# The head of an S5 state-space plus SwiGLU kernel: one activation for the inverse deviation, gate and up weights loaded three feature tiles at a time, and the second chunk of x held back by a GpSimd write

## The chip, the cores and the metric

The kernel runs on one core of a Trainium2 chip. A core has TensorE (PE, matrix products; PEld is its weight load, which overlaps the products), VectorE (DVE), ScalarE (ACT), GpSimd (POOL) and SyncE (SP, which here only issues DMAs). Sixteen DMA engines carry the transfers that SP, ACT and POOL issue, each from its own queue. The metric is the device time of one execution in microseconds (us); the profile shows one execution and its span, which leaves out a little around the work.

## The reference

The input x has 2048 rows of 512 numbers in bf16. It is layer-normalized, and the output is the sum of x and two branches on the normalized rows xn:

```python
xn = _layernorm(x, axis=-1)                       # (x - mean) / sqrt(var + 1e-5)
return x + A(xn) + B(xn)

# A: diagonal complex state space, 512 states
dt = exp(log_dt); Lam = Lambda_re + 1j * Lambda_im
Lam_bar = exp(dt * Lam);  B_bar = ((Lam_bar - 1.0) / Lam)[:, None] * (B_re + 1j * B_im)
h_t = Lam_bar * h_(t-1) + B_bar @ xn_t
y_t = 2.0 * real(Cmat @ h_t) + xn_t * Dskip

# B: feed-forward with 1376 features
(silu(xn @ w_gate) * (xn @ w_up)) @ w_down
```

## The kernel before

**Tiling.** The rows are 16 token tiles of 128 (`NT`), in four chunks of 512 (`CW`, four tiles each, `TPC`). The 512 columns are four slices of 128 (`KD`). The 1376 features are ten tiles of 128 and a last one of 96. `xnT` holds xn transposed, the moving operand of all products on the input side. A gate or up product of a feature tile and a chunk is four matmuls of 512 columns (one per slice), a tile of the state space's input (`bproj_tile`, stationary operand `BT`, real part and imaginary part) is four as well.

**The head.** For chunk 0 the work goes token tile by token tile, so that TensorE can start before all of x is there: `ln_stats` (DVE: bn_stats and bn_aggr, variance and mean), `rstd_act` (ACT: Ln and Exp, lines 206 and 207), `norm_dve` (DVE, line 219), `xT_pe` (four TensorE transposes by an identity, line 236, and two copies from PSUM on DVE or ACT, lines 243 and 245), then `head_mm` (line 696): gate and up matmuls of 128 columns of the first three feature tiles, gathered in six PSUM banks (`held`). `dummy` issues matmuls on ones to keep TensorE busy before there is work. After the head, `gu_out` applies Silu on ACT and copies the up half. The order is written out by hand; each engine runs its instructions in the order of the code and waits by semaphores.

**After the head.** Feature tiles 3 to 6 of chunk 0 (line 448), the eight `bproj_tile`s of chunk 0 (line 373), feature tiles 7 to 9 and the last one, then chunk 1 and so on. Beside that, a backlog of DVE and ACT work (`queue`, `pump`, `need`) is handed out by estimated costs: the layer norm of the next chunk (tag ln1: four statistics, a power on POOL for rstd, four normalizations, each followed by a DMA transpose), the sine and cosine tables (`table_ops`), the scans.

**Loads.** `fgroups` cuts the gate and up weights into groups of feature tiles, (0, 2), (2, 3), (3, 7), (7, 10), each one tile in SBUF (`wg0`, `wu0` and so on) with one DMA (`load_w1`, line 112). SP's queue issues in this order: x tile 0, gate group 0, x tile 2, gate and up group 1, x tiles 4 to 7 in two DMAs (line 137), gate and up group 2, the four DMA transposes of B's real part (line 142), gate and up group 3, the four of its imaginary part, the last feature tile's weights, then the DMA transposes of chunk 1 (line 250) and the later loads. ACT's queue issues x tile 1, up group 0, x tile 3. POOL's queue loads the three parameter rows of the state space. A DMA is issued only when the earlier one that used its semaphore has landed.

**Parameters.** `prm_transpose` (in `xT_pe(2)`) turns the three parameter rows, `params_a` and `params_a2` compute dt = exp(log_dt) and r = exp(dt * Lambda_re) on ACT and load the table for Silu and Sin, `params_sin` reduces angles to turns on DVE and takes two sines on ACT.

Of the kernel before, what the change touches and what calls it, by code (L numbers as in the profile page):

```python
# [10 lines left out]
F32 = mybir.dt.float32  # L11
# [5 lines left out]
MAGIC = 12582912.0  # L17
# [6 lines left out]
def kernel(  # L24
# [63 lines left out]
    fgroups = [(0, 2), (2, 3), (3, 7), (7, FT - 1)]  # L88
# [41 lines left out]
    load_w1(nc.sync, wg_g, wg_v, 1)  # L130
    load_w1(nc.sync, wu_g, wu_v, 1)
# [4 lines left out]
    for n in (TPC, TPC + 2):  # L136
        nc.sync.dma_start(out=xall[:, n:n + 2, :], in_=x_v[:, n:n + 2, :])
    load_w1(nc.sync, wg_g, wg_v, 2)
    load_w1(nc.sync, wu_g, wu_v, 2)
    for part, src in enumerate((A_B_re, A_B_im)):  # L140
        for k in range(KD):
            nc.sync.dma_start_transpose(out=BT[:, part, k, :], in_=src[:, k * 128:(k + 1) * 128])
        if part == 0:
            load_w1(nc.sync, wg_g, wg_v, 3)
            load_w1(nc.sync, wu_g, wu_v, 3)

    nc.sync.dma_start(out=w_last[:, :, 0:LB + LA], in_=wg_v[:, :, FL:F])
    nc.sync.dma_start(out=w_last[:, :, LB + LA:128], in_=wu_v[:, :, FL + LB:F])

# [38 lines left out]

    stats = const.tile([128, NT, 6], F32, name="stats")
    mv = const.tile([128, NT, 2], F32, name="mv")  # L190
# [13 lines left out]
    def rstd_act(n):  # L204

        nc.scalar.activation(out=ve[:, n:n + 1], in_=mv[:, n, 1:2], func=ACT.Ln, bias=eps_t[:, 0:1])
        nc.scalar.activation(out=rstd[:, n:n + 1], in_=ve[:, n:n + 1], func=ACT.Exp, scale=-0.5)
# [9 lines left out]
    def norm_dve(n):  # L217
        c, i = divmod(n, TPC)
        nc.vector.tensor_scalar(out=xn_tile(c)[:, i, :], in0=xall[:, n, :], scalar1=mv[:, n, 0:1],  # L219
                                scalar2=rstd[:, n:n + 1], op0=ALU.subtract, op1=ALU.mult)  # L220
# [93 lines left out]
    def params_sin():  # L314

        def turns(dst, shift):
            src = ws2[:]
            if shift:
                V.tensor_scalar(out=dst[:], in0=src, scalar1=shift, scalar2=None, op0=ALU.add)
                src = dst[:]  # L320
            V.tensor_scalar(out=kk[:], in0=src, scalar1=MAGIC, scalar2=MAGIC, op0=ALU.add, op1=ALU.subtract)
            tt(dst[:], src, kk[:], ALU.subtract)

        V.tensor_scalar(out=ws2[:, 1, :], in0=ws2[:, 0, :], scalar1=float(CW), scalar2=None, op0=ALU.mult)
        turns(fs1, 0.0)
        nc.scalar.activation(out=sin1[:], in_=fs1[:], func=ACT.Sin, scale=TWO_PI_LO)
        turns(fc1, 0.25)
# [554 lines left out]
```

## Time and profile before

| | |
|---|---|
| median of 3 runs | 179.12 us (179.03 to 179.21) |
| profiled execution | 179.15 us, of which its span 177.4 us |
| busy share of the span | PE 97%, DVE 87%, ACT 53%, PEld 47%, POOL 21% |
| chain that ended last | PE 96%, DMA 1%, DVE 1% |
| granted TensorE clock | full |
| read and written in HBM | 8.42 MB and 5.24 MB, 77 GB/s over the span |

The busy share of an engine is an average over the whole span. The chain that ended last follows the work back from the last instruction, at each step to what released it. A line of the timeline gives the start, the length, the engine, the line of the code, the operation, what is written and read, how many instructions are merged, and in brackets how long the engine sat idle before and what ended that. PEq, SPq and ACTq are the sequencers that issue. An issue on SPq is only the issue: the transfer lands later, and the table of DMA issues gives the time from issue to landing.

### The profile page before, as it was taken

How to read it: one execution, taken by the hardware profiler on the slowest of the kernel's cores; microseconds unless marked ns; L12 is line 12 of the kernel's file. 1: busy time of each engine (PE TensorE's matmuls, PEld its weight loads, DVE VectorE, ACT ScalarE, POOL GpSimd, SP SyncE). 2: the span in 40 equal slices, each digit the busy share in tenths (PEclk: the TensorE clock that was granted, in tenths of full speed). 3: DMA queues.
4: the chain of work that ended last, by engine and by line, in shares of the span. 5: the costliest groups of instructions: out<-in, count | busy, mean ns of one | idle time of the engine just before them, and what ended most of it. 6: DMA issues, size and time to landing. Idle time of an engine off the chain costs nothing.

```text
span 177.4 us, 2512 instructions
## 1 busy us (share of the span) xinstructions
PE 172.8 (97%) x921; PEld 83.0 (47%) x921; DVE 154.8 (87%) x239; ACT 94.8 (53%) x173; POOL 37.6 (21%) x57
## 2 busy tenths in 40 slices
PE   7899999999999999999999999999999999999993
PEld 2784444444444444444444444444444444464443
DVE  6789997999999977899999999999999999992033
ACT  3579696977399459924966662013866610001300
POOL 6003000001200040000706640005183720001410
PEclk9999999999999999999999999999999999999999
DMA  5999748983041025900460011005569600000662
GB/s 158 311 274 239 147 90 245 342 135 89 0 89 33 0 40 107 355 0 0 43 79 9 15 51 42 0 0 59 59 79 184 113 8 0 0 0 4 64 103 71
DMA packets 30092, 16.13 MB, mean 91 GB/s; under 512 B 19296, under 2 KB 29888, under 8 KB 30048
## 3 DMA queue, kind: packets, MB, share of 16 engines
q1 hardware_dynamic: 24416, 11.41, 28.1%
q0 software_dynamic: 4416, 3.87, 16.1%
q10 hardware_dynamic: 1248, 0.69, 1.4%
q8 instruction: 7, 0.11, 0.3%
q14 instruction: 5, 0.04, 0.1%
HBM read 8.42 MB, written 5.24 MB: 77 GB/s over the span
## 4 chain that ended last, share of the span: by engine, by line
PE 96%; DMA 1%; DVE 1%; issue 0%
PE ps L448 36%; PE ps L608 16%; PE ps L373 16%; PE ps L561 10%; PE ps L589 10%; PE ps L696 3%; PE ps L503 2%; DMA xall<-in_A_x_dram 1%; PE ps L492 1%; PE ps L596 1%; PE ps L549 1%; PE ps L236 1%; DVE stats L201 0%; DVE stats L703 0%; DVE xall L219 0%; DVE res L613 0%
## 5 line engine op out<-in xcount | busy, mean ns | idle before, releaser
L448 PE MATMUL ps<-xnT,wu 128*128 128x512 bf16 x148 | 38.0, 379 | 0.0
L448 PE MATMUL ps<-xnT,wg 128*128 128x512 bf16 x148 | 38.0, 379 | 0.0
L415 DVE TENSOR_TENSOR_SCAN g<-r_t,car,u 128x512 bf16<-128x512 f32 x24 | 28.8, 1262 | 0.0
L373 PE MATMUL ps<-xnT,BT 128*128 128x512 bf16 x128 | 28.3, 379 | 0.0
L608 PE MATMUL ps<-CF,wt 128*128 128x512 bf16 (+2 forms) x144 | 28.2, 355 | 0.0
L462 ACT ACTIVATE guT<-ps 128x512 bf16<-128x512 f32 x40 | 24.6, 615 | 5.0 <-PE ps L448 4.9
L463 ACT CAST u<-ps 128x512 bf16<-128x512 f32 x40 | 24.1, 601 | 5.2 <-PE ps L448 5.0
L620 ACT CAST res<-ps 128x512 bf16<-128x512 f32 x12 | 6.8, 594 | 37.5 <-PE ps L608 37.5
L621 POOL DMA_DIRECT2D out_dram<-res x12 | 10.7, 1062 | 59.4 <-ACT res L620 59.4
L448 PEld LDWEIGHTS <-wu 128*128 128x128 bf16 x148 | 14.5, 98 | 17.5
L448 PEld LDWEIGHTS <-wg 128*128 128x128 bf16 x148 | 14.5, 98 | 17.2
L608 PEld LDWEIGHTS <-wt 128*128 128x128 bf16 x144 | 13.3, 98 | 14.9 <-issue 0.8
L375 ACT CAST u<-ps 128x512 bf16<-128x512 f32 x32 | 17.7, 589 | 3.6 <-PE ps L373 3.6
L373 PEld LDWEIGHTS <-BT 128*128 128x128 bf16 x128 | 12.5, 98 | 15.1
L589 PE MATMUL ps<-wd_sb,guT 128*128 128x512 bf16 x80 | 18.1, 379 | 0.0
L561 PE MATMUL ps<-wd_sb,guT 128*128 128x512 bf16 (+1 forms) x90 | 17.6, 355 | 0.0
L211 POOL TENSOR_TENSOR rstd<-ve,neg_half 128x4 f32<-128x4 f32 x3 | 5.3, 1763 | 54.1 <-DVE ve L210 54.1
L186 POOL DMA_DIRECT2D gu_rows<-gu_last x24 | 12.0, 506 | 10.3 <-DVE gu_last L479 9.0
L467 DVE TENSOR_TENSOR guT<-guT,u 128x1024 bf16<-128x1024 bf16 x20 | 13.5, 679 | 0.0
L561 PEld LDWEIGHTS <-guT 128*128 128x128 bf16 x90 | 8.8, 98 | 8.7
L589 PEld LDWEIGHTS <-guT 128*128 128x128 bf16 x80 | 7.8, 97 | 9.5
L613 DVE TENSOR_TENSOR res<-ps,xn_end 128x512 bf16<-128x512 f32 (+1 forms) x4 | 2.5, 625 | 10.6 <-PE ps L608 10.6
(116 smaller groups left out, 196.1 us busy)
## 6 DMA issues: line engine op xcount, KB each, us to landing
out_dram<-in_A_x_dram SPq DMA_DIRECT2D x1, 1536.0 KB, 7.1
out_dram<-res POOLq DMA_DIRECT2D x12, 128.0 KB, 3.2
out_dram<-xall POOLq DMA_DIRECT2D x3, 512.0 KB, 7.8
wd_sb<-in_B_w_down_dram SPq DMA_DIRECT2D x1, 1280.0 KB, 10.2
xall<-in_A_x_dram SPq DMA_DIRECT2D x1, 1024.0 KB, 6.5
xall<-in_A_x_dram SPq DMA_DIRECT2D x2, 256.0 KB, 4.7
wg<-in_B_w_gate_dram SPq DMA_DIRECT2D x1, 512.0 KB, 5.4
wu<-in_B_w_up_dram SPq DMA_DIRECT2D x1, 512.0 KB, 6.3
```

The lines of the kernel that those rows point to most:

```text
L186: nc.gpsimd.dma_start(out=gu_rows[c % 2][i * RT:(i + 1) * RT, p, :], in_=gu_last[c % 3][p * RT:(p + 1) * RT, i * 128:(i + 1) * 128])
L373: nc.tensor.matmul(ps[:], lhsT=BT[:, part, k, q * 128:(q + 1) * 128], rhs=xnT[:, k, c * CW:(c + 1) * CW], start=(k == 0), stop=(k == KD - 1))
L375: nc.scalar.copy(out=u_tiles[c][:, part, q, :], in_=ps[:])
L415: V.tensor_tensor_scan(out=g()[:, part, q, :], data0=r_t[:, q:q + 1].to_broadcast([128, CW]), data1=u_tiles[c][:, part, q, :], initial=ini ...
L448: nc.tensor.matmul(ps[:fs, lo:hi], lhsT=wslice(groups, fi, k), rhs=xnT[:, k, c * CW + lo:c * CW + hi], start=(k == 0), stop=(k == KD - 1))
L462: nc.scalar.activation(out=guT[:fs, fi, :], in_=psg[:fs], func=ACT.Silu)
L463: nc.scalar.copy(out=u_pair[c][:fs, fi % 2, :], in_=psu[:fs])
L467: products.append(lambda: V.tensor_tensor(out=g, in0=g, in1=u, op=ALU.mult))
L561: nc.tensor.matmul(o[:, lo:hi], lhsT=gu_tiles[k][:, fi, i * 128:(i + 1) * 128], rhs=wd_sb[:, fi, lo:hi], start=(fi == 0), stop=False)
L589: nc.tensor.matmul(o[:], lhsT=gu_tiles[c][:, fi, i * 128:(i + 1) * 128], rhs=wd_sb[:, fi, lo:hi], start=(fi == 0), stop=False)
L608: nc.tensor.matmul(o, lhsT=w_tiles[c][:, part, q, i * 128:(i + 1) * 128], rhs=CF[:, part, q, lo:hi], start=(fresh and part == 0 and q == 0 ...
L621: nc.gpsimd.dma_start(out=out_v[:, n, :], in_=res[:], accum_op=ALU.add)
```

## The change

- The head's rstd is one ACT instruction, Abs_reciprocal_sqrt of the variance with the epsilon as bias, in place of Ln and Exp; the activation table loaded at the start is another, and the table for Silu and Sin is loaded right after the head's last rstd.
- The first weight groups are (0, 3), (3, 7), (7, 10): three feature tiles in the first gate load and in the first up load, no loads of a single tile. The head computes all three feature tiles token tile by token tile.
- x tile 1's statistics are taken in two halves, with tile 0's normalization between them. Eight dummies of 512 columns and two of 128 stand in place of nine of 512.
- Token tiles 4 to 7 are loaded by four DMAs, and they come behind a GpSimd write of two numbers, read from gate group 0, into the place of tile 4; so SP issues tile 4, and all that stands behind it in its order, when gate group 0 has landed.
- The two exponentials of the parameters are powers of e on GpSimd, the parameter transpose moves from `xT_pe(2)` to `xT_pe(3)`, the turns (`params_turns`) are the first item of the tables in the backlog, the two sines a later one.

```diff
-    fgroups = [(0, 2), (2, 3), (3, 7), (7, FT - 1)]
+    fgroups = [(0, 3), (3, 7), (7, FT - 1)]
...
-    eps_t = const.tile([128, 1], F32, name="eps_t")
-    nc.vector.memset(eps_t[:], EPS)
-    nc.scalar.preload_act_table_set("natural_log_exp_and_others")
+    nc.scalar.preload_act_table_set("abs_reciprocal_sqrt_and_small")
...
     nc.sync.dma_start(out=xall[:, 2, :], in_=x_v[:, 2, :])
     nc.scalar.dma_start(out=xall[:, 3, :], in_=x_v[:, 3, :])
-    load_w1(nc.sync, wg_g, wg_v, 1)
-    load_w1(nc.sync, wu_g, wu_v, 1)
...
-    for n in (TPC, TPC + 2):
-        nc.sync.dma_start(out=xall[:, n:n + 2, :], in_=x_v[:, n:n + 2, :])
-    load_w1(nc.sync, wg_g, wg_v, 2)
-    load_w1(nc.sync, wu_g, wu_v, 2)
...
+    e_t = const.tile([128, NQ], F32, name="e_t")
     ident = const.tile([128, 128], BF16, name="ident")
     make_identity(nc, ident[:])
+    nc.gpsimd.memset(e_t[:], float(np.e))
...
+    nc.gpsimd.tensor_copy(out=xall[0:1, TPC, 0:2], in_=wg_g[0][0:1, 0, 0:2])
+    for n in range(TPC, 2 * TPC):
+        nc.sync.dma_start(out=xall[:, n, :], in_=x_v[:, n, :])
+    load_w1(nc.sync, wg_g, wg_v, 1)
+    load_w1(nc.sync, wu_g, wu_v, 1)
+    for part, src in enumerate((A_B_re, A_B_im)):
+        for k in range(KD):
+            nc.sync.dma_start_transpose(out=BT[:, part, k, :], in_=src[:, k * 128:(k + 1) * 128])
+        if part == 0:
+            load_w1(nc.sync, wg_g, wg_v, 2)
+            load_w1(nc.sync, wu_g, wu_v, 2)
...
     def rstd_act(n):
-        nc.scalar.activation(out=ve[:, n:n + 1], in_=mv[:, n, 1:2], func=ACT.Ln, bias=eps_t[:, 0:1])
-        nc.scalar.activation(out=rstd[:, n:n + 1], in_=ve[:, n:n + 1], func=ACT.Exp, scale=-0.5)
+        nc.scalar.activation(out=rstd[:, n:n + 1], in_=mv[:, n, 1:2], func=ACT.Abs_reciprocal_sqrt, bias=EPS)
...
     def params_a(pp):
         V.tensor_copy(out=prm[:].rearrange("p t q -> p (t q)"), in_=pp[:, 0:3 * NQ])
-        nc.scalar.activation(out=dt_t[:], in_=ldt, func=ACT.Exp)
-    def params_a2():
-        V.tensor_tensor(out=dre[:], in0=dt_t[:], in1=lre, op=ALU.mult)
-        nc.scalar.activation(out=r_t[:], in_=dre[:], func=ACT.Exp)
-        nc.scalar.preload_act_table_set("silu_and_others")
+        nc.gpsimd.tensor_tensor(out=dt_t[:], in0=e_t[:], in1=ldt, op=ALU.pow)
+        nc.gpsimd.tensor_tensor(out=dre[:], in0=dt_t[:], in1=lre, op=ALU.mult)
+        nc.gpsimd.tensor_tensor(out=r_t[:], in0=e_t[:], in1=dre[:], op=ALU.pow)
+    def params_turns():
...
         V.scalar_tensor_tensor(out=ws2[:, 0, :], in0=dt_t[:], scalar=INV_2PI, in1=lim, op0=ALU.mult, op1=ALU.mult)
+        V.tensor_scalar(out=ws2[:, 1, :], in0=ws2[:, 0, :], scalar1=float(CW), scalar2=None, op0=ALU.mult)
+        turns(fs1, 0.0)
+        turns(fc1, 0.25)
...
     allk = range(KD)
-    dummy(9, CW)
+    dummy(8, CW)
+    dummy(2, 128)
     ln_stats(0)
     rstd_act(0)
-    nc.vector.bn_stats(out=stats[:, 1, :], in_=xall[:, 1, :])
+    nc.vector.bn_stats(out=stats_1[:, 0, :], in_=xall[:, 1, 0:D // 2])
     norm_dve(0)
-    nc.vector.bn_aggr(out=mv[:, 1, :], in_=stats[:, 1, :])
+    nc.vector.bn_stats(out=stats_1[:, 1, :], in_=xall[:, 1, D // 2:D])
+    nc.vector.bn_aggr(out=mv[:, 1, :], in_=stats_1[:])
     rstd_act(1)
     xT_pe(0, on_dve=(0,))
     dummy(4, 128)
     norm_dve(1)
     ln_stats(2)
-    head_mm(0, 0, 1, range(0, HK), (0, 1))
-    head_mm(0, 0, 1, range(HK, KD), (0, 1))
+    kh = (range(0, HK), range(HK, KD))
+    fis = range(H)
+    head_mm(0, 0, 1, kh[0], fis)
+    head_mm(0, 0, 1, kh[1], fis)
     xT_pe(1)
     rstd_act(2)
-    head_mm(1, 0, 1, range(0, HK), (0, 1))
-    head_mm(1, 0, 1, range(HK, KD), (0, 1))
+    head_mm(1, 0, 1, kh[0], fis)
+    head_mm(1, 0, 1, kh[1], fis)
...
     rstd_act(3)
-    head_mm(0, 1, 2, range(0, HK), (0, 1))
-    head_mm(1, 1, 2, range(0, HK), (0, 1))
-    head_mm(0, 1, 2, range(HK, KD), (0, 1))
-    head_mm(1, 1, 2, range(HK, KD), (0, 1))
-    head_mm(0, 0, 2, allk, (2,))
-    pp = xT_pe(2, on_dve=(0, 1), prm_too=True)
-    head_mm(1, 0, 2, allk, (2,))
+    nc.scalar.preload_act_table_set("silu_and_others")
+    head_mm(0, 1, 2, kh[0], fis)
+    head_mm(0, 1, 2, kh[1], fis)
+    xT_pe(2, on_dve=(0, 1))
+    head_mm(1, 1, 2, allk, fis)
     norm_dve(3)
+    head_mm(0, 2, 3, kh[0], fis)
+    head_mm(1, 2, 3, kh[0], fis)
+    pp = xT_pe(3, on_dve=(0, 1), prm_too=True)
     params_a(pp)
-    params_a2()
...
-    queue("tables", tables[:2])
+    queue("tables", [(1.0, params_turns)] + tables[:2])
     queue("ln1", norm1)
-    queue("tables", tables[2:])
+    queue("tables", tables[2:4] + [(0.1, params_sin)] + tables[4:])
```

More of the change, by code (lines that the diff above doesn't have):

```diff
@@ L187, in move_rows @@
                                     in_=gu_last[c % 3][p * RT:(p + 1) * RT, i * 128:(i + 1) * 128])
+    nc.gpsimd.tensor_copy(out=xall[0:1, TPC, 0:2], in_=wg_g[0][0:1, 0, 0:2])
[9 more added lines that the diff above has]
+            load_w1(nc.sync, wu_g, wu_v, 2)
+    nc.sync.dma_start(out=w_last[:, :, 0:LB + LA], in_=wg_v[:, :, FL:F])
+    nc.sync.dma_start(out=w_last[:, :, LB + LA:128], in_=wu_v[:, :, FL + LB:F])
     stats = const.tile([128, NT, 6], F32, name="stats")
+    stats_1 = const.tile([128, 2, 6], F32, name="stats_1")
     mv = const.tile([128, NT, 2], F32, name="mv")
@@ L215, in ln_nb, with norm_dve @@
                                        op0=ALU.mult, op1=ALU.mult)
-    def norm_dve(n):
+    def norm_dve(n, lo=0, hi=D):
         c, i = divmod(n, TPC)
-        nc.vector.tensor_scalar(out=xn_tile(c)[:, i, :], in0=xall[:, n, :], scalar1=mv[:, n, 0:1],
+        nc.vector.tensor_scalar(out=xn_tile(c)[:, i, lo:hi], in0=xall[:, n, lo:hi], scalar1=mv[:, n, 0:1],
                                 scalar2=rstd[:, n:n + 1], op0=ALU.subtract, op1=ALU.mult)
```

33 lines of the change are left out of this document (9 added, 24 removed).

## The prediction

> **What bounds the kernel now.** I read the page's shares first (PE busy 97% of the span), then the chain that ended last in order of time, because a share cannot say where the other 3% lies.
>
> ```profile
> 5.11 0.40 PE ps L236 x4
> ...
> 5.78 0.62 PE ps L696 x8
> ...
> 12.09 6.91 PE ps L448 x32
> 18.99 6.91 PE ps L373 x32
> ```
>
> Columns: start, length, what. Before these lines the path is the load of the first x tile, its statistics and normalization up to 5.06, and from 5.11 TensorE alone until 174.6. Whatever starts TensorE earlier is won in full; whatever makes it wait anywhere later is lost in full.
>
> Second, the timeline around the first normalization, which is what the new rstd touches:
>
> ```profile
> 4.08 0.29 ACT L206 ACTIVATE ve<-mv,eps_t 128x1 f32<-128x1 f32 x1 [2.06 <-DVE mv L202]
> 4.41 0.20 ACT L207 ACTIVATE rstd<-ve 128x1 f32<-128x1 f32 x1
> 4.64 0.41 DVE L219 TENSOR_SCALAR xall<-xall,mv,rstd 128x512 bf16<-128x512 bf16 x1
> ```
>
> Third, SP's issues, and the table of DMA issues (last column: microseconds from issue to landing):
>
> ```profile
> 3.24 1.81 SPq L137 DMA_DIRECT2D xall<-in_A_x_dram  x2
> 5.09 0.47 SPq L112 DMA_DIRECT2D wg<-in_B_w_gate_dram  x1
> 5.84 0.37 SPq L112 DMA_DIRECT2D wu<-in_B_w_up_dram  x1
> 6.25 5.76 SPq L142 DMA_TRANSPOSE BT<-in_A_B_re_dram  x4
> ...
> 12.57 0.75 PEld L448 LDWEIGHTS <-wu 128*128 128x128 bf16 x4
> ```
> ```profile
> wg<-in_B_w_gate_dram SPq DMA_DIRECT2D x1, 512.0 KB, 5.4
> wu<-in_B_w_up_dram SPq DMA_DIRECT2D x1, 512.0 KB, 6.3
> wg<-in_B_w_gate_dram SPq DMA_DIRECT2D x1, 384.0 KB, 4.6
> wu<-in_B_w_up_dram SPq DMA_DIRECT2D x1, 384.0 KB, 6.1
> ```
>
> The up weights of tiles 3 to 6 are issued at 5.84 and land at 12.1; TensorE loads the first of them at 12.57. That slack of 0.4 to 0.5 us is the narrowest on the input side, and the loads are bound by bandwidth (337 to 349 GB/s from 7 to 11 us). Last, slices of half a microsecond (us, busy time of PE, PEld, DVE, ACT, POOL, clock, DMA share, GB/s) and the instruction queue of the slice from 12.3 to 12.4:
>
> ```profile
> 12.00:12.50 0.50, 0.50 (x5) 0.22 (x3) 0.47 (x3) 0.50 (x2) 0.00 (x0) 1.00 1.44 291
> 12.50:13.00 0.50, 0.50 (x4) 0.20 (x2) 0.47 (x3) 0.50 (x2) 0.00 (x0) 1.00 5.39 168
> 13.00:13.50 0.50, 0.50 (x4) 0.26 (x3) 0.50 (x2) 0.50 (x2) 0.00 (x0) 1.00 0.02 2
> 13.50:14.00 0.50, 0.50 (x4) 0.23 (x3) 0.47 (x3) 0.50 (x2) 0.00 (x0) 1.00 0.08 9
> 14.00:14.50 0.50, 0.50 (x4) 0.19 (x2) 0.47 (x2) 0.50 (x2) 0.00 (x0) 1.00 0.71 154
> ```
> ```profile
> q8 instruction: 1, 0.02, 68.2%
> ```
>
> At 12.35 TensorE's instruction stream is refilled by one 16,384-byte packet, and from 12.78 to 14.23 nearly nothing moves, with transposes in the queue. At 17.21 another instruction fetch is followed, from 17.66 to 18.58, by 8 GB/s; the 384 KB up load whose last data packet started at 17.2 landed only at 18.8 (the 6.1 above). At 34.27 a third is followed by a standstill from 35.1 to 36.8. Before the change all three fall where TensorE waits for nothing.
>
> **The change, part by part.** The profiled run took 179.15 us with a span of 177.4; the median shown is 179.12, so I sum against 179.15 and lower the result by 0.03.
>
> *One activation for rstd.* Ln and Exp cost 0.29 and 0.20, and with hand-overs 4.08 to 4.61. One activation lies between these rows, done at 4.31 to 4.40; I take 4.40, the row with an added epsilon. DVE must also be past the half-width statistics of tile 1: the full one is 0.66, a half lies between 0.33 and 0.66, I take 0.40 (a part of an instruction does not shrink: a 128x6 aggregate still takes 0.18). Started at 3.96 it is out of the way by 4.4. So normalization starts at 4.40 instead of 4.64, the first transposes at 4.87 instead of 5.11. The second half (0.40) and its aggregate (0.18) now stand ahead of the copy of the transposed tile on DVE: 4.73, 5.17, copy at 5.27 instead of 5.44, first head matmul at 5.60 instead of 5.78. Gain 0.18; bounds 0 (a half costs as much as a whole) and 0.33 (halves at 0.33, rstd at 0.20). Dropping one long dummy for two short ones frees TensorE at about 4.06 instead of 4.17, before it is needed either way.
>
> *Three feature tiles at once.* Matmul columns are the same: 96 of 128 against 80 of 128 and 8 of 256; at 56 ns per 128 columns that adds under 0.03 us. Before tile 2's transposes there are now 40 units of 128 columns instead of 44, so TensorE gets there at 7.84, while tile 2's normalization (statistics after tile 1's normalization at 6.05, 0.69 + 0.18, rstd behind two ACT copies until 7.15, 0.41 on DVE) ends at about 7.9. About 0.05 of the gain goes there; up to 0.3 if x tile 2 lands late. The gain that reaches tile 3 is 0.15 (bounds 0 and 0.33).
>
> *Parameters and sines.* Exp of 0.21 twice becomes two POOL powers; the nearest row is the 128x4 power at 1.5 to 1.8 us. With the product, r and dt are there by about 14.5, POOL being idle until the power of ln1 (14.96 before). Their first users on DVE come behind ln1's four statistics (four times 0.84 from 10.9, so 14.2). Cost nothing while DVE has that queue; if not, 1.5 us of DVE, which TensorE does not wait for here. The earlier Silu table load (1.28 us) covers an ACT without work; before, it held the first Silu back to 11.71.
>
> *The hold.* The first gate load grows from 256 to 384 KB, landed 1.20 + 3.5 = 4.7 before. 128 KB more at half of 340 GB/s (the ACT queue takes the other half) is 0.77: 5.4, just ahead of its first use at 5.55 (bounds 4.7 and 5.8). The POOL write costs 0.1 like POOL's small memsets, nothing is behind it on POOL until the powers at 10.8, and x tile 4 is issued at 5.6 instead of 3.24. Behind it in SP's order stand three x tiles, both weight loads, the B transposes, everything later. Four x issues at 0.5 (rows 0.40 to 0.53) put the gate load at 7.6, the up load at 8.1 instead of 5.84, the first transpose at 8.6 instead of 6.25. Packets start about 1.0 after an issue (the first x tile: issue 0.74, first packet 1.8), so the DMA engines, done with the first group near 6.0, idle until 6.6, then run at the pace of the x issues until 8.6, then carry 1 MB at 340 GB/s until 11.7. With 0.5 to 0.7 from last packet to landing (0.69 for the same load before) the up weights land at 12.2 to 12.4. TensorE, 0.15 earlier, wants them at 12.4 and can take them 0.1 later without a gap: by this alone no loss, bounds -0.0 and +0.4.
>
> *The refill.* Up to the fetch at 12.35 TensorE had issued 121 weight loads: 13 dummies, 17 transposes, 88 of the head, 3 of tile 3. Now 14 + 17 + 96 = 127 stand ahead of tile 3, so the 121st is six before the end of the head: 11.87 - 0.15 - 6 x 0.056 = 11.4. By the row at 12.35 movement stops 0.43 later, at 11.8, and comes back 1.88 after the fetch, at 13.3. The up load's last packets start at 11.6 to 11.7 with the transposes right behind: the pattern of 17.21, whose landing was held. So landing at about 13.35. Before, the weights could be loaded at 12.67 at the latest (matmul at 12.79); now at 13.38: +0.7, the head's gain used up in it. Ends: no hold at all (-0.15), and the third case's 2.58 from fetch to movement (14.0: +1.3).
>
> [...]
>
> *Later loads.* SP runs 2.3 behind at the B transposes, 1.5 behind at their second half, which was issued by 18.99 and landed at 20.9. Its last tile is then there by 22.3; TensorE needs it at 22.9. Covered by 0.6; if that cover goes, the loss is what is missing. The transposes of chunk 1 (landing 26.7, used at 31.9) have 5 us.
>
> Sum: 179.15 + 0.7 - 0.03 = 179.8.
>
> **Rivals.**
>
> *Up weights in time.* If the standstill touches only transposes (at 34.27 plain loads ran on at 298 to 369 GB/s until they ended at 34.75), or the up load is done before 11.8, the landing stays at 12.2 to 12.4, and the end is earlier by the head's 0.15: 179.0. It decides where the landing is before 12.67; for slower by over 0.2% (0.36 us, about what a measurement here can tell) it must pass 13.0. Against it: the held landing of 18.8. A refill that costs nothing ends here too, with 0.15 of the 0.36. Chance 0.36, with small delays up to 0.36.
>
> *Faster beyond 0.2%.* All low ends in the head, 0.33, and no wait later: 178.8, at the edge. Chance 0.06.
>
> *B's second half late.* Wider spacing of the transposes (1.53 each instead of 1.26) and a standstill near 19 put its last tile at 23.5 to 24.0: +0.6 to +1.1 over 22.9, up to 180.6 with the forecast's stall partly inside. Chance 0.06.
>
> **How the numbers follow.** Forecast 0.52, its own range 179.5 to 180.5. Faster 0.06, same 0.36, slower 0.52 + 0.06 = 0.58. The range runs from 178.9 (the in-time case with 0.25) to 180.5 (the longest standstill seen), leaving about 0.1 on each side.
>
> **What would show it.** Right: first transposes near 4.87, first head matmul near 5.6, x tile 4 issued near 5.6, the instruction packet near 11.4, DMA at a few GB/s after 11.8, TensorE idle before tile 3's up weights for about 0.8 us. Wrong: that load landing before 12.6, no idle time on TensorE after 5.6, or idle time at the B matmuls.

## The result and the profile after

The changed kernel takes 179.83 us (median of 9 runs, 179.46 to 180.4), the kernel before 179.06 us on the same chip (9 runs, 178.97 to 179.42). The ratio is 1.0035, with a 95% interval of 1.0023 to 1.0046: slower by 0.77 us by the medians and by 0.6 (0.4 to 0.8) by the ratio. The profiled execution, 179.47 us with a span of 177.7 us, lies at the low end of its own nine and 0.32 above the profiled 179.15 of before, so it shows only 0.32 of these 0.77 us. What it shows of places is read as such, with its own sizes; the size of the whole loss is read from the medians, and where an execution at the median loses the rest, no profile shows.

The chain that ended last, in order of time, for the kernel after (start, length, what):

```profile
1.52 5.10 DMA wu<-in_B_w_up_dram
6.62 0.05 issue
6.67 1.51 PE ps L693 x24
8.20 0.40 PE ps L235 x4
...
12.22 7.07 PE ps L445 x32
19.30 6.91 PE ps L370 x32
```

Before, the chain went through the first x tile and was TensorE's own from 5.11 on. Now one load fills it from 1.52 to 6.62: the head's up weights, issued at 1.52, landed at 6.62. From 6.67 on TensorE leads again. The two later lines answer to those at 12.09 and 18.99 of before: the same work, 0.31 later at 19.30.

The timeline of the kernel after, around the places that the prediction named (start, length, engine, line, what, and in brackets the idle time and what ended it):

```profile
3.82 0.20 ACT L206 ACTIVATE rstd<-mv 128x1 f32<-128x1 f32 x1 [1.79 <-DVE mv L202]
4.05 0.41 DVE L218 TENSOR_SCALAR xall<-xall,mv,rstd 128x512 bf16<-128x512 bf16 x1
4.52 0.40 PE L235 MATMUL ps<-ident,xall 128*128 128x128 bf16 x4
4.79 0.18 POOL L173 COPY xall<-wg 1x2 bf16<-1x2 bf16 x1 [0.48 <-DMA wg<-in_B_w_gate_dram]
4.99 1.82 SPq L175 DMA_DIRECT2D xall<-in_A_x_dram  x4
5.25 0.84 PE L693 MATMUL ps<-xnT,wg 128*128 128x128 bf16 x12
6.67 0.84 PE L693 MATMUL ps<-xnT,wu 128*128 128x128 bf16 x12 [0.36 <-DMA wu<-in_B_w_up_dram]
6.85 0.43 SPq L112 DMA_DIRECT2D wg<-in_B_w_gate_dram  x1
7.33 0.51 SPq L112 DMA_DIRECT2D wu<-in_B_w_up_dram  x1
12.06 1.03 PE L445 MATMUL ps<-xnT,wg 128*128 128x512 bf16 x4
13.07 0.55 PEld L445 LDWEIGHTS <-wu 128*128 128x128 bf16 x4 [0.48 <-DMA wu<-in_B_w_up_dram]
13.08 1.04 PE L445 MATMUL ps<-xnT,wu 128*128 128x512 bf16 x4
```

and three lines of the kernel before, its first up matmuls of the head, and tile 3's gate and up matmuls:

```profile
6.47 0.61 PE L696 MATMUL ps<-xnT,wu 128*128 128x128 bf16 x8
...
11.92 1.03 PE L448 MATMUL ps<-xnT,wg 128*128 128x512 bf16 x4
12.79 1.03 PE L448 MATMUL ps<-xnT,wu 128*128 128x512 bf16 x4
```

The new rstd is one instruction of 0.20, and the first head matmul stands at 5.25 instead of 5.78. At 6.67 TensorE has waited 0.36 for the head's up weights, and its up matmuls, at 6.47 before, are now 0.20 behind. At 13.07 the weight load of tile 3's up half has waited 0.48 for the load issued at 7.33. TensorE loses less than that there, because the matmuls of the gate half were still running: the up matmuls start 1.02 after the gate's (13.08 and 12.06), before 0.87 (12.79 and 11.92). So the profiled execution is late by 0.14 at the start of tile 3 and by another 0.16 at tile 3's up weights. After that nothing more is lost: the last matmul ends at 174.88, before at 174.58.

Slices of the kernel after (us, busy time of PE, PEld, DVE, ACT, POOL, granted clock, DMA share, GB/s):

```profile
8.00:8.50 0.50, 0.49 (x10) 0.31 (x8) 0.23 (x2) 0.22 (x2) 0.00 (x0) 1.00 0.83 137
8.50:9.00 0.50, 0.50 (x13) 0.50 (x11) 0.48 (x3) 0.50 (x1) 0.00 (x0) 1.00 0.82 152
9.00:9.50 0.50, 0.50 (x13) 0.50 (x11) 0.33 (x2) 0.50 (x1) 0.00 (x0) 1.00 0.78 266
9.50:10.00 0.50, 0.50 (x13) 0.50 (x11) 0.00 (x0) 0.27 (x1) 0.00 (x0) 1.00 1.06 369
...
11.50:12.00 0.50, 0.50 (x12) 0.50 (x10) 0.50 (x1) 0.50 (x2) 0.42 (x2) 1.00 2.91 271
12.00:12.50 0.50, 0.50 (x8) 0.26 (x5) 0.47 (x3) 0.50 (x2) 0.42 (x2) 1.00 0.90 105
12.50:13.00 0.50, 0.50 (x3) 0.09 (x1) 0.47 (x3) 0.50 (x2) 0.50 (x1) 1.00 0.68 136
```

and the instruction queue of the same kernel in the slice from 12.15 to 12.25:

```profile
q8 instruction: 1, 0.02, 100.4%
```

The view names no engine for this queue; that it feeds TensorE is the author's reading, and its seven packets in the kernel before, 102 to 135 weight loads apart, agree with it.

Two stretches are slow. One at 11.75 to 12.75 looks like the standstill that the prediction counted on, and tile 3's up weights land at its end, at 13.03. The other, at 8.0 to 9.0, was in no part of the prediction. And the instruction fetch starts at 12.19, when the standstill had already begun. So the wait at tile 3 was forecast, but it cost 0.16 and not 0.7, the order of events speaks against the cause given for it, and the wait at 6.67 was not forecast at all.

### The profile page after: what moved, and what is told of

The parts are those of the page before. It is cut to its first block, busy times and chain, and to the rows that moved or that the text cites. A ratio compares the mean times of both kernels' runs of the same rounds, so it can differ in the third digit from the quotient of the medians.

```text
span 177.7 us, 2527 instructions
## 1 busy us (share of the span) xinstructions
PE 173.5 (98%) x930; PEld 83.2 (47%) x930; DVE 154.6 (87%) x238; ACT 94.1 (53%) x167; POOL 39.5 (22%) x62
## 3 DMA queue, kind: packets, MB, share of 16 engines
HBM read 8.42 MB, written 5.24 MB: 77 GB/s over the span
## 4 chain that ended last, share of the span: by engine, by line
PE 95%; DMA 3%; ACT 0%; DVE 0%; issue 0%
PE ps L445 36%; PE ps L605 16%; PE ps L370 16%; PE ps L558 10%; PE ps L586 10%; DMA wu<-in_B_w_up_dram 3%; PE ps L693 3%; PE ps L500 2%; PE ps L489 1%; PE ps L593 1%; PE ps L546 1%; ACT L118 0%; PE ps L235 0%; DVE res L610 0%; PE ps L265 0%
## 5 line engine op out<-in xcount | busy, mean ns | idle before, releaser
L618 POOL DMA_DIRECT2D out_dram<-res x12 | 10.5, 1043 | 59.4 <-ACT res L617 59.4
L370 PEld LDWEIGHTS <-BT 128*128 128x128 bf16 x128 | 12.5, 98 | 15.1
L210 POOL TENSOR_TENSOR rstd<-ve,neg_half 128x4 f32<-128x4 f32 x3 | 4.8, 1607 | 45.9 <-DVE ve L209 45.0
```

The lines of the kernel that those rows point to most:

```text
L370: nc.tensor.matmul(ps[:], lhsT=BT[:, part, k, q * 128:(q + 1) * 128], rhs=xnT[:, k, c * CW:(c + 1) * CW], start=(k == 0), stop=(k == KD - 1))
L618: nc.gpsimd.dma_start(out=out_v[:, n, :], in_=res[:], accum_op=ALU.add)
```

## The experiments

The theory to test was the prediction's: the refill of TensorE's instructions stops the DMA engines just before tile 3's up weights have landed. Its rivals: the DMA transposes of B, queued right behind that load, stop it; or the load is late by itself, because the hold starts it late and it moves slowly at first; or the loss lies in the head, in the larger up load. All times are medians in us, and the comparisons are with runs of the kernel before on the same chip. None of these kernels leaves work out.

| kernel | time (range, runs) | ratio to before, 95% |
|---|---|---|
| after, again | 179.68 (179.43 to 179.94, 12) | 1.0026 (1.0015 to 1.0036) |
| e1 transposes later | 179.87 (179.32 to 180.51, 12) | 1.0038 (1.0025 to 1.0052) |
| e2 refill earlier | 180.67 (179.74 to 181.68, 6) | 1.0084 (1.0053 to 1.0116) |
| e3 no hold | 180.06 (179.76 to 180.39, 6) | 1.0046 (1.0031 to 1.0061) |
| e4 head alone | 179.16 (178.87 to 179.9, 12) | 0.9996 (0.9983 to 1.0009) |
| e4h, hold ahead of the identity | 180.09 (179.74 to 181.94, 11) | 1.0061 (1.0036 to 1.0086) |
| e5 weights first | 179.67 (179.41 to 180.0, 9) | 1.0026 (1.0016 to 1.0037) |
| e6 x in two loads | 180.04 (179.71 to 180.35, 6) | 1.0044 (1.003 to 1.0059) |
| e7 hold, two-tile groups | 179.92 (179.44 to 180.74, 8) | 1.0049 (1.0032 to 1.0066) |
| e7 again | 179.71 (179.38 to 180.69, 11) | 1.0039 (1.0024 to 1.0055) |
| e8 hold, weights first | 181.27 (180.38 to 181.62, 6) | 1.0107 (1.0085 to 1.013) |
| e9 up load cut | 180.02 (179.93 to 180.14, 5) | 1.0046 (1.0034 to 1.0059) |

**The change once more**, unaltered, for a second profile.

> The changed kernel once more, unaltered, to see how much of its loss moves from execution to execution. Both theories (a standstill of the DMA engines caused by TensorE's instruction refill; a standstill caused by B's transposes arriving behind the up load) expect 179.8 +- 0.2 in the middle, a wait of TensorE before the head's up weights and another before tile 3's up weights, together 0.5 to 1.2 us. If the waits sum to the same in each execution, the spread of 179.46 to 180.4 comes from somewhere else.

179.68, and the profiled execution 179.52. Its waits on the input side:

```profile
PE ps L693 <- DMA wu<-in_B_w_up_dram: 0.2, 1, 0.2
PEld L693 <- DMA wu<-in_B_w_up_dram: 0.4, 1, 0.4
PEld L445 <- DMA wu<-in_B_w_up_dram: 0.3, 1, 0.3
```

The same two places: the head's up load (landed 6.83) and tile 3's (13.06). Their prices are others: tile 3 starts 0.31 later than before, and its up matmuls lose only 0.02 more. The slow stretch is there again (123 and 154 GB/s in the two slices from 8.0). The fetch is at 12.80 this time, behind the first slow slice of the standstill (212 GB/s from 12.0), 0.6 later than in the first profile, and still the weights land at the same time.

**e1: B's transposes behind the next weights.** In SP's order gate and up group 2 go ahead of the transposes of B's real part.

```diff
     load_w1(nc.sync, wu_g, wu_v, 1)
+    load_w1(nc.sync, wg_g, wg_v, 2)
+    load_w1(nc.sync, wu_g, wu_v, 2)
     for part, src in enumerate((A_B_re, A_B_im)):
...
-        if part == 0:
-            load_w1(nc.sync, wg_g, wg_v, 2)
-            load_w1(nc.sync, wu_g, wu_v, 2)
```

> B's four real-part transposes are issued behind the third gate and up groups, so plain loads alone follow tile 3's up weights. Transpose theory: no standstill at 11.8, those weights land at 11.7 to 12.4, no wait at tile 3, 179.3 to 179.6; the wait before the head's up weights stays. Refill theory: the standstill stays near 11.8 to 12.7, the weights land at 12.9 or later, the time is that of the changed kernel, 179.7 to 180. B's second half must land by 22.9; it is issued no later than before and should.

179.87: no gain. Slices, columns as above:

```profile
8.00:8.50 0.50, 0.50 (x13) 0.50 (x11) 0.50 (x3) 0.00 (x0) 0.00 (x0) 1.00 0.65 125
8.50:9.00 0.50, 0.50 (x13) 0.50 (x11) 0.15 (x2) 0.38 (x2) 0.00 (x0) 1.00 0.88 127
...
12.50:13.00 0.50, 0.45 (x5) 0.25 (x3) 0.50 (x2) 0.50 (x3) 0.42 (x2) 1.00 1.09 367
13.00:13.50 0.50, 0.50 (x3) 0.03 (x2) 0.47 (x3) 0.50 (x3) 0.50 (x1) 1.00 1.06 338
13.50:14.00 0.50, 0.50 (x3) 0.26 (x4) 0.50 (x1) 0.50 (x3) 0.12 (x1) 1.00 1.16 364
14.00:14.50 0.50, 0.50 (x4) 0.21 (x3) 0.43 (x4) 0.50 (x3) 0.00 (x0) 1.00 2.31 297
```

The standstill before 13 is gone, the engines run at 338 to 367 GB/s, and yet tile 3's up weights land at 13.43 (fifteen of their sixteen parts by 12.95), no earlier than in the change. So in this kernel neither the refill nor the transposes hold that load. What is left is the load itself, and in it the slow stretch at 8.0 to 9.5: against 340 GB/s its three slices (125, 127 and, from 9.0, 197) are short of 285 KB, which is 0.84 us at 340 GB/s. The fetch, at 13.64 here, falls into plain loads, and they go on at 364 and 297 GB/s.

The packets in the traces say the same of the change itself. The last packet of these weights ends at 12.39 there, and the load has landed 0.64 later; in e1, with no transposes behind the load, the two are 12.80 and 13.43, and in the kernel before 11.49 and 12.12, 0.63 apart in both. So the standstill adds nothing to the landing that can be seen. Its held packets are released at 12.77, after the last packet of the weights: it looks like the transposes' wait for that load, and not like the load's wait for them.

This kernel also waits 0.4 us on the weight load's side for the second half of B, which the reordering delayed (the prediction's third rival, by another road), of which only 0.07 reaches the last matmul, and 0.8 in the head, whose up load landed at 7.21 here.

**e2: the refill moved.** 34 short dummies instead of eight long and two short: 24 more weight loads ahead of the head, by which the author expected the fetch earlier.

```diff
-    dummy(8, CW)
-    dummy(2, 128)
+    dummy(34, 128)
```

> The ten warm-up matmuls (8 of 512 columns, 2 of 128) are 34 of 128 columns, the same TensorE time in 24 more instruction pairs, so the first refill comes about 24 x 0.056 = 1.3 us earlier in the head, near 10.8 instead of 12.2, while plain loads alone are moving. Refill theory: no standstill holds tile 3's up weights, or it comes at 11.2 and holds them less; landing 12.2 to 12.5, 179.2 to 179.6; and the second standstill of 13.0 to 14.4 is gone. Transpose theory: the standstill at 11.8 stays where it is, landing near 13.0, 179.7 to 180.

180.67. The packet was fetched at 11.87, only 0.3 earlier than in the change, whose own two profiles differ by 0.6, so the count of weight loads does not set the fetch alone. The standstill is at 12.0 to 12.9, here behind the fetch, and tile 3's up weights land at 13.27. The refill was hardly moved, so this is a weak test, and e3 is the stronger one. The profiled execution, 179.74, is the fastest of the six and does not show what made the median so long. It shows one new effect, the twelve first head matmuls at half pace:

```profile
5.33 1.48 PE L693 MATMUL ps<-xnT,wg 128*128 128x128 bf16 x12
```

**e3: no hold.** The GpSimd write is left out; order and groups stay as in the change.

```diff
-    nc.gpsimd.tensor_copy(out=xall[0:1, TPC, 0:2], in_=wg_g[0][0:1, 0, 0:2])
```

> The GpSimd write is taken out, nothing else, so x tile 4 and all behind it are issued from 2.2 on, and only semaphores of earlier loads hold them. If the hold is what makes tile 3's up weights late, they land at 11.4 to 12.0, the wait there is gone, and the time falls to 179.0 to 179.4. Against that, x tiles 4 to 7 and the second gate group then share the DMA engines with the head's up weights on ACT's queue, which by sharing alone land 0.3 to 0.5 later than 6.6, so the first wait grows to 0.7 to 0.9. If the two cancel, the time stays at 179.7 to 180.

180.06; the profiled execution, 180.39, the slowest of its six, has its whole loss in the head:

```profile
PE ps L692 <- DMA wu<-in_B_w_up_dram: 1.3, 1, 1.3
PEld L692 <- DMA wu<-in_B_w_up_dram: 1.5, 1, 1.5
```

Its slices, and its instruction queue in the slice from 12.1 to 12.3:

```profile
8.00:8.50 0.50, 0.50 (x13) 0.50 (x11) 0.31 (x1) 0.00 (x0) 0.00 (x0) 1.00 1.03 348
8.50:9.00 0.50, 0.50 (x13) 0.50 (x11) 0.50 (x2) 0.00 (x0) 0.00 (x0) 1.00 1.10 369
...
10.50:11.00 0.50, 0.50 (x13) 0.50 (x11) 0.00 (x0) 0.33 (x1) 0.00 (x0) 1.00 2.09 278
11.00:11.50 0.50, 0.50 (x13) 0.50 (x10) 0.36 (x2) 0.00 (x0) 0.00 (x0) 1.00 1.18 119
11.50:12.00 0.50, 0.50 (x12) 0.50 (x10) 0.50 (x3) 0.00 (x0) 0.14 (x1) 1.00 0.92 200
```
```profile
q8 instruction: 1, 0.02, 32.9%
```

Without the hold there is no slow stretch at 8. The standstill comes at 10.5 to 11.6, together with the first transposes, and the fetch follows only at 12.15. So this first standstill does not come from the refill. Tile 3's up weights land at 11.95 and nothing waits for them. But the head's up load, which now shares the engines with four x tiles and the next megabyte of weights, lands at 7.68 instead of 6.62 (fourteen of its sixteen parts by 6.97). In these two profiles the hold brings the first landing forward by 1.06 and puts the second off by 1.08; TensorE gains by that, as the second has slack: its last matmul ends at 174.88 with the hold and at 175.77 without.

**e4: the head's arithmetic alone.** The kernel before with the single rstd activation, the halved statistics, the dummies, and the parameters on GpSimd; loads, groups and their order as before, no hold.

```diff
-        nc.scalar.activation(out=ve[:, n:n + 1], in_=mv[:, n, 1:2], func=ACT.Ln, bias=eps_t[:, 0:1])
-        nc.scalar.activation(out=rstd[:, n:n + 1], in_=ve[:, n:n + 1], func=ACT.Exp, scale=-0.5)
+        nc.scalar.activation(out=rstd[:, n:n + 1], in_=mv[:, n, 1:2], func=ACT.Abs_reciprocal_sqrt, bias=EPS)
...
-    nc.vector.bn_stats(out=stats[:, 1, :], in_=xall[:, 1, :])
+    nc.vector.bn_stats(out=stats_1[:, 0, :], in_=xall[:, 1, 0:D // 2])
     norm_dve(0)
+    nc.vector.bn_stats(out=stats_1[:, 1, :], in_=xall[:, 1, D // 2:D])
```

> The kernel before with the new arithmetic of the head alone: one activation for rstd, the split statistics, the shorter warm-up, the parameters on GpSimd. Loads, their groups and the order of the head's matmuls are as before, nothing is held. Theory L (the whole loss comes from the loads: three feature tiles in the first groups, and the hold): TensorE starts 0.25 to 0.5 us earlier, the head's up weights land at 6.1 as before and tile 3's at 12.1; they are wanted at 12.2, so 178.7 to 178.95 against 179.1. Rival A (the arithmetic itself costs, through GpSimd powers of 1 us or DVE's order): 179.1 to 179.4.

179.16 against 179.18: no difference. Its first head matmul stands at 5.37 in the profiled execution, 0.41 earlier than before, and by the medians it is worth nothing. The head's up weights do not come earlier with it: before, they landed at 6.08 and were used at 6.47, so 0.39 was the most that any earlier start could win unless they come earlier too. In the profiled execution of e4, the slowest of its twelve (179.9), they were a full microsecond late:

```profile
7.23 0.62 PE L694 MATMUL ps<-xnT,wu 128*128 128x128 bf16 x8 [0.97 <-DMA wu<-in_B_w_up_dram]
```

The load is the same 256 KB as before. Its 16 completion marks came in from 4.84 to 7.18, in the profile before from 5.55 to 6.08: one of its sixteen parts was late (the fifteenth was in by 6.19), not the load as a whole. What the usual executions of e4 wait for, no profile shows.

**e4h and e7: the hold with the groups of before.** Both are e4 with the GpSimd write ahead of x tiles 4 to 7 and of what follows them.

```diff
+    nc.gpsimd.tensor_copy(out=xall[0:1, TPC, 0:2], in_=wg_g[0][0:1, 0, 0:2])
     for n in (TPC, TPC + 2):
         nc.sync.dma_start(out=xall[:, n:n + 2, :], in_=x_v[:, n:n + 2, :])
```

In e4h the write stands ahead of the identity on GpSimd:

> The same as the head alone, with the GpSimd write ahead of x tiles 4 to 7 added; the first groups stay at two feature tiles, the single third tile is loaded ahead of the hold. If the hold by itself makes the slow stretch of 60 to 170 GB/s that the held kernels show from 8.0 to 9.2 us, tile 3's up weights land at 12.7 to 13.2 instead of 12.1 and the time is 179.1 to 179.6. If the stretch needs the three-tile groups too, the time is that of the head alone, 178.7 to 178.95.

180.09, but not a fair test: the identity was queued behind the waiting write, and TensorE waited 0.7 us for it ahead of the first transposes (5.24 instead of 4.5 to 4.6). One thing it does show: tile 3's up weights land at 13.23 and cost TensorE 0.40, although the three slices from 8.0 run at 324, 303 and 311 GB/s. That load can be late without the slow stretch. In e7 the write stands behind the identity and the iota, as in the change:

> The kernel before with the new arithmetic of the head, the first groups of two feature tiles and the third apart as before, and the GpSimd write ahead of x tiles 4 to 7, this time behind the identity and the ramp on GpSimd, so that it keeps nothing of the head waiting. If three tiles in the first loads are what costs, the head's up weights (256 KB) land at 5.8 to 6.1, in time, and tile 3's at 12.4 to 12.9 for the hold: 178.9 to 179.3. If the hold is what costs, 179.4 to 179.9 as with the three-tile groups.

179.92, and 179.44 for the profiled execution, in which the first use of tile 3's up weights waited 0.4 on the weight load's side, of which 0.06 reached the matmuls. That did not account for a median 0.85 above before, where e4's is level with it, hence a second profiled execution of the same kernel:

> The kernel of the hold with two-tile groups, unaltered, for a second profiled execution: its median was 179.92 but its profiled execution 179.44, with 0.4 us of waiting before tile 3's up weights and 0.2 us in the head. If its usual loss is tile 3's up weights, a profiled execution near 179.9 shows a wait of 0.7 to 1.0 us there (landing 12.8 to 13.1). If it is the head's up load on ACT's queue, the wait is 0.5 to 0.9 us at the first up matmuls of the head and tile 3's is 0.4 or less. If it is neither, the two together stay under 0.6 us and the rest is found later, at the matmuls of B.

179.71; the profiled execution 179.67. None of the three fits whole: the two waits are 0.3 each and together stay under 0.6, as the third has it, but nothing is lost at the matmuls of B. The end of its chain, below the span:

```profile
core 0 of [0], span 177.9 us
...
174.60 0.02 issue
174.62 0.29 DVE res L612
```

and the same of the kernel before:

```profile
core 0 of [0], span 177.4 us
...
174.59 0.02 issue
174.62 0.29 DVE res L613
```

TensorE and VectorE end at the same moment as before, and the span is 0.5 us longer. The extra time lies in the closing part, in which SP collects the engines (in the kernel before from 175.31 on) and the semaphores are cleared (there at 176.89): 3.3 us from the last matmul to the end of the span in e4h, in both profiles of e7 and in e9; 2.8 to 2.9 in all others, the kernel before (2.80) and the change (2.82) among them. In e4h and e7 the 0.5 us stand between two neighbouring instructions of SP. Why there, no run shows. If it is the same in the executions without a profile, 0.5 of the 0.85 and 0.55 us by which e7's two medians lie above before is no effect of the hold on the work: with two-tile groups the hold then costs about 0.1 to 0.4 by the medians, and in the two profiled executions the last matmul ends 0.17 earlier than before and at the same time. Tile 3's up weights land at 12.56 and 12.68 there, in the change at 13.03 and 13.06.

**e5: the weights ahead of x.** The held write goes into gate group 1, whose loads stand ahead of x tiles 4 to 7.

```diff
-    nc.gpsimd.tensor_copy(out=xall[0:1, TPC, 0:2], in_=wg_g[0][0:1, 0, 0:2])
-    for n in range(TPC, 2 * TPC):
-        nc.sync.dma_start(out=xall[:, n, :], in_=x_v[:, n, :])
+    nc.gpsimd.tensor_copy(out=wg_g[1][0:1, 0, 0:2], in_=wg_g[0][0:1, 0, 0:2])
     load_w1(nc.sync, wg_g, wg_v, 1)
     load_w1(nc.sync, wu_g, wu_v, 1)
+    for n in range(TPC, 2 * TPC):
+        nc.sync.dma_start(out=xall[:, n, :], in_=x_v[:, n, :])
```

> The changed kernel with the GpSimd write put into the second gate group's place instead of x tile 4's, and the second gate and up groups issued ahead of x tiles 4 to 7. Tile 3's up weights then have 1 MB ahead of them after the hold instead of 1.5 MB: even with a slow stretch they land near 11, wanted at 12.5. The wait at tile 3 goes (0.15 to 0.5 us), the wait before the head's up weights stays: 179.2 to 179.6. If tile 3's wait was only a shift of the first one, no change: 179.7 to 179.9. x tiles 4 to 7 come 1.5 us later, wanted from 10.6 on by VectorE only; that may delay its backlog without reaching TensorE.

179.67, the change's own time. The wait at tile 3 is gone, so it is a matter of when that load starts. In its place the profiled execution (180.0) waits 0.4 for the head's gate weights and 0.4 for x tile 2 to be normalized, tile 3 starts at 12.45, 0.4 later than in the change, and another 0.29 is lost between 32 and 58 us. The slow stretch moves along with the weight load: it is now at 7.0 to 8.0 (68 and 117 GB/s), behind a pause from 6.0 on in which the DMA engines had little to do (a share of 0.42 and 0.20).

**e6: two x loads instead of four** in the held part, as before.

```diff
-    for n in range(TPC, 2 * TPC):
-        nc.sync.dma_start(out=xall[:, n, :], in_=x_v[:, n, :])
+    for n in (TPC, TPC + 2):
+        nc.sync.dma_start(out=xall[:, n:n + 2, :], in_=x_v[:, n:n + 2, :])
```

> The changed kernel with x tiles 4 to 7 in two loads of 256 KB, as before, instead of four of 128 KB; the hold stays. SP then issues the second gate load about 0.9 us earlier (5.9 instead of 6.85). If the slow stretch comes from SP's issues falling behind the DMA engines, the up weights land 0.5 to 0.9 earlier, 179.3 to 179.6. If it comes from the engines having run dry and slow rings catching up, the landing moves by less than 0.3 and the time stays at 179.6 to 179.9.

180.04. The weight loads are issued at 5.92 and 6.43, 0.9 earlier, and the up weights land at 13.53, not earlier at all: the slow stretch is there (117 and 193 GB/s in the two slices from 8.0), and the parts of the gate load ahead of them land over 2.2 us, from 9.87 to 12.11. So SP's pace of issue, which the prediction charged with 2 us, does not set the landing.

**e8: e7 with the third tile's and tile 3's weights held and x behind them.**

```diff
-    nc.gpsimd.tensor_copy(out=xall[0:1, TPC, 0:2], in_=wg_g[0][0:1, 0, 0:2])
-    for n in (TPC, TPC + 2):
-        nc.sync.dma_start(out=xall[:, n:n + 2, :], in_=x_v[:, n:n + 2, :])
+    nc.gpsimd.tensor_copy(out=wg_g[1][0:1, 0, 0:2], in_=wg_g[0][0:1, 0, 0:2])
+    load_w1(nc.sync, wg_g, wg_v, 1)
+    load_w1(nc.sync, wu_g, wu_v, 1)
     load_w1(nc.sync, wg_g, wg_v, 2)
     load_w1(nc.sync, wu_g, wu_v, 2)
+    for n in (TPC, TPC + 2):
+        nc.sync.dma_start(out=xall[:, n:n + 2, :], in_=x_v[:, n:n + 2, :])
```

> As the previous one, but the GpSimd write goes into the third feature tile's gate weights and the order behind it is: third tile, second large gate and up groups, x tiles 4 to 7, B. Only the first tiles of x and the two-tile groups are in flight until 4.7. Up weights of the head at 5.7 to 6.0, third tile at 7.3 (wanted at 7.7), tile 3's up weights at 11 to 11.5 (wanted at 12.2), x tile 4 at 12.5 (wanted by VectorE at 10.7, which does not reach TensorE). If waits on loads are the whole of what the head's new arithmetic lacks, 178.6 to 178.9; if the time of the clock's release or TensorE's own order is what holds, 179.0 to 179.3.

181.27, the worst, with the best head of all: no wait for weights, tile 3 at 11.61. Its waits in the first 60 us:

```profile
DVE stats L203 <- DMA xall<-in_A_x_dram: 3.0, 2, 2.4
...
PEld L447 <- issue: 2.0, 2, 1.3
```

x tile 4 lands at 12.5, VectorE stands still for 2.4 us, and its backlog, which fed TensorE just in time, reaches TensorE between 49 and 54 us. The second chunk's x is not free to wait.

**e9: the head's up load cut** into 256 KB for two feature tiles and 128 KB for the third, both on ACT's queue.

```diff
+    ugroups = [(0, 2), (3, 7), (7, FT - 1), (2, 3)]
...
     load_w1(nc.scalar, wu_g, wu_v, 0)
+    load_w1(nc.scalar, wu_g, wu_v, 3)
```

> The changed kernel with the up half of its first group cut in two on ACT's queue: 256 KB for feature tiles 0 and 1, then 128 KB for tile 2. If the size of that load is what the wait before the head's up matmuls consists of (0.2 to 0.8 us in the runs so far), it shrinks to 0 to 0.3, since the first two tiles land 0.4 to 0.8 earlier, and the time falls to 179.3 to 179.6 unless tile 3's up weights then wait for themselves, which caps the gain at about 0.3. If the wait comes from one lagging DMA engine whatever the size, it stays: 179.6 to 179.9.

180.02. There is no wait ahead of the head's up matmuls, but TensorE asked for them only at 7.02, having run the first gate matmuls at half pace (1.46 us for the twelve), so the time shows nothing of the cut itself. The landing does: the 256 KB part landed at 6.91, no earlier than the 384 KB of the change (6.62 and 6.83), though fifteen of its sixteen parts were in by 6.15. Here one late part set the landing, as the second branch of the expectation has it, and not the size. Tile 3's gate half starts at 12.42, and 0.5 us of the total is the closing part.

**Taken together.** Counted at the last matmul's end in the profiles, before is 174.58, the two-tile groups with the hold 174.41 and 174.58, the three-tile groups with the hold 174.88 and 174.90, the three-tile groups without it 175.77. The larger first loads, with the order of the head and the four x loads that come with them, are what costs: 1.2 us in one profiled execution (e3 against before) and 0.9 by the medians (e3 against e4). The landing of the head's up load points the same way: with the hold, the load of 256 KB landed at 5.96 to 6.48 in four profiles and that of 384 KB at 6.61 to 7.21 in six; e9's part of 256 KB, at 6.91, is the exception. Tile 3's up weights cost TensorE 0.16 and 0.02 in the two profiles of the change and 0 to 0.40 in the others, so what is lost up to the start of tile 3 is about as much or more in the change (0.14 and 0.31), and all of it in e3 (1.19). The hold gives some of it back, in the head, and takes a part again at tile 3: by the medians 0.2 to 0.4 remain as its gain (the change against e3). No kernel was faster than before; e4 equals it.

## Why the prediction was right, and where it was not

The number, the direction and one of the two places were right: 179.83 against 179.8, tile 3's up weights at 13.03 against 13.35, TensorE waiting for them. The cause given for it was wrong, and so was the price: of the 0.7 us that the sum puts at tile 3, the two profiles show 0.16 and 0.02. The rest of what they show, 0.14 and 0.31, lay in a place that the prediction did not look at, and what the medians lose beyond that, 0.2 to 0.5, no profile places. So the total fits by luck.

*One activation for rstd.* Mechanism right, gain larger than priced. rstd took 0.20, the lower of the two rows between which it was put; the half statistics took the 0.40 assumed. The first transposes came at 4.52 (4.87 forecast), the first head matmul at 5.25 (5.60): 0.53 earlier than before. Of that 0.26 lies ahead of the new arithmetic, for x tile 0 had landed at 2.85 instead of 3.11 (2.81 to 3.02 in all profiles but that of before; why, no run shows), and 0.27 is the gain to set against 0.18.

*Three feature tiles at once.* This step failed. It let 0.15 of the gain reach tile 3; instead tile 3 began 0.14 later than before (12.06 against 11.92). The missing term is the up load of the head: the prediction priced the growth of the first gate load (5.4 forecast, 4.73 measured) and its first use, and never that of the up load beside it, which grew by as much on ACT's queue. It landed at 6.62 and 6.83 in the two profiles of the change, and was wanted at 6.3 and 6.7. What to look at was in the trace before: landed at 6.08, used at 6.47, so 0.39 was all the cover there was, for a smaller load and a later head; the 0.4 to 0.5 at tile 3, which the prediction took for the narrowest slack, is no narrower. The one profile of e4 shows the same limit without any change to the loads.

*Parameters and sines.* Right: nothing. The powers on GpSimd took 1.05 and 1.01, less than the 1.5 to 1.8 of the nearest row.

*The hold.* The times of issue were a little pessimistic (x tile 4 at 4.99 for 5.6, the gate load at 6.85 for 7.6, the up load at 7.33 for 8.1), the landing was too early: 12.2 to 12.4 forecast without a refill, 13.03 measured. The term that failed is the rate, 340 GB/s from 8.6 on. Measured are 137, 152 and 266 GB/s in the three slices from 8.0 to 9.5, short by 232 KB, or 0.68 us at 340. That much later than 12.2 to 12.4 is 12.9 to 13.1. The agreement is loose: the forecast counted from issues about 0.8 later than they came, though e6 shows that 0.9 of earlier issue brings nothing, and e4h has the load late without the slow stretch.

*The refill.* This step failed as a cause. The fetch came at 12.19, behind 129 weight loads, instead of 11.4, behind the 121 counted before; the standstill had begun at 11.75. e3 has the standstill 1.6 us ahead of the fetch, e1 has the fetch without a standstill of the plain loads (364 and 297 GB/s), and the weights late all the same. In the change the landing follows the last packet by 0.64, in e1 without the standstill by 0.63, so the standstill does not put it off. That the landing came near 13.35 is chance: a missing rate term of 0.68 stood in for the 0.95 to 1.15 that the refill was given. That the loss came out at 0.7 is chance as well: a landing 0.9 later than before cost TensorE 0.16, as the gate half's matmuls ran on meanwhile and tile 3 itself began later.

*Later loads.* Right for the change: B's second half was in time. e1, which delays it, waited 0.4 on the weight load's side and lost 0.07.

*The rivals.* The profiled execution alone, 0.32 above that of before, would have gone to the rival of weights in time with small delays; the medians, 0.77 and 0.55 above before in the two comparisons, decide against it.

**Open.** What makes the first microsecond of the second weight load slow. It is there in every kernel with the hold and three-tile groups, goes along with the load when that stands ahead of x (e5), and comes in e8 too; it is absent without a hold (e3) and with the groups of before and x first (e4h, e7). Neither SP's pace (e6) nor the transposes (e1) make it. The packets narrow it down: from 8.0 to 9.0 of the change 14 of the 141 packets of 1024 bytes took 0.2 to 0.88 us, most of the others about 0.05 as ever, so single packets are held and the rest run at their usual pace. Such packets (over 0.2 us, from 5.0 to 13.2) number 0, 1 and 5 in the kernels without the hold (e4, before, e3) and 9 to 33 in those with it. What holds them, no run shows. Open too is where an execution at the median loses the 0.2 to 0.5 us that the two profiles of the change do not have.

## What to carry to other kernels

When a load grows, price the landing and the first use of every load that grows with it, on every queue: an engine that starts earlier only wins up to the slack of the next thing it needs, which the profile shows as landing and first use (here 6.08 and 6.47). A wait of the weight load is not yet a loss: 0.48 of waiting cost the matmuls 0.16, so price the next matmul's start. A suspected cause has to come before its effect, in the trace of a second kernel too: here a wrong cause gave the right number. And before a difference of half a microsecond is put down to an edit, subtract the closing part of the span, which differed by 0.5 us between kernels whose work ended at the same time.

## What the runs showed of the chip that was not expected

- **The moment from which TensorE runs at full pace differs from one execution to the next.** The same twelve matmuls of 128 columns took 0.84 (after), 1.12 (after again), 0.95 (e5), 1.46 (e9) and 1.48 us (e2): one starts every 0.107 us at half pace and every 0.056 at full pace. The full pace began between 3.4 us (before) and 6.7 us (e2), while the granted clock in the slices reads 1.00 throughout. Two profiles of one kernel differ by 1.8 (4.1 and 5.9 in the change). Where that moment comes no earlier, a head that starts earlier has more of its matmuls at half pace: in e2, from 5.33 on, all of these twelve. The spread is 3.3 us over all kernels and 1.8 within one; what sets the moment, no run shows.
- **One load's sixteen completion marks can lie far apart.** The head's up load: 0.5 us from first to last before, 1.0 in the change, 2.1 in e3, 2.3 in e4, where TensorE waited 1.0 for it. No run here shows what makes one of them late.
- **A standstill of about a microsecond as the DMA transposes begin behind plain loads**, ahead of the refill in some kernels (10.5 to 11.6 in e3, 11.75 to 12.75 in the change) and behind it in others (12.0 to 12.9 in e2, from 14.25 in e1). In the thirteen profiles other than e1's, the held packets are released 0.2 to 0.4 us after the last packet of the plain loads ahead of them has ended (12.39 and 12.77 in the change, 11.31 and 11.68 in e3). A second one follows after the fetch has begun (13.2 to 14.65 in the change, 12.6 to 14.1 in e3).
- **The closing part of the program is 2.8 or 3.3 us**, the same in both profiles of one kernel (2.82 and 2.84 for the change, 3.26 and 3.33 for e7).
